# Earlier weight splits, three pieces a step beside the last routing, and exps ahead of the second tile's split

## The chip, the core and the metric

The kernel runs on one core of a Trainium2 chip. The metric is the time of one execution on the device, in microseconds (us), as the median of several runs. TensorE (PE) multiplies matrices, VectorE (DVE), ScalarE (ACT) and GpSimd (POOL) work on elements, and SP issues most of the DMA transfers, in the order in which they stand in its program, each when what it waits for is there.

## What is computed

Sliding-window attention over 4 sequences of 576 tokens, 8 heads of 64, then a mixture of 8 experts of which each token takes the two with the highest noisy logits, then a SwiGLU block behind an RMS norm. Cut to what matters here:

```python
scores = scale * np.matmul(q, k.transpose(0, 1, 3, 2))          # attention, window of 128
attn = np.exp(scores - max); attn = attn / attn.sum()
x = matmul(attn, v)                                             # 2304 tokens x 512
noisy_logits = x @ w_gate + np.log1p(np.exp(x @ w_noise)) * noise
top2 = np.argpartition(-noisy_logits, 2, axis=1)[:, :2]
for e in range(E):                                              # 8 experts
    h = np.maximum(x[mask] @ w1[e], 0.0)                        # 512 -> 1024
    out[mask] += top2_w[mask, k, None] * (h @ w2[e])            # 1024 -> 512
y = (silu(xn @ w_gate2) * (xn @ w_val) @ w_out)                 # xn: RMS norm of out
```

## The kernel before

The 2304 tokens are 18 tiles of 128. Float32 numbers go to TensorE as two float16 parts, a high one (a ScalarE copy) and a low one (a subtraction on VectorE or GpSimd); this is what "split" means below, for q and k of a tile (`split`, L262), for the result x (`split_x`, L379) and for the experts' weights (`weight_steps`, L98).

The attention loop (`while n < NS + HP + 2 ...`) runs in steps `n`, each one pair of heads of one tile: four steps a tile, 72 in all, from `n` = -2 on. A step writes out, for every engine in its order, the scores of steps `n + 2` and `n + 3` (TensorE L319, every second step), the turning of step `n`'s exps (L347), the products with v of step `n - 2` (L361), the exps of step `n + 1` (ScalarE L339), the shift and row minimum of step `n + 2` (VectorE L330), and beside them small work: loads of q, k and v (`load_qkv`, `load_v`), splits of tiles two ahead, `split_x` and `put_x` of a finished tile, logits (L458) and the routing of a batch of tiles (`route`, a generator that does one part a step: exp and ln, maxima and their indices, one-hots `m`, rank matmuls L495 and L497, then `slots`). The scheduler reorders nothing here (`manual_schedule`): each engine runs its instructions as the code writes them, and waits where something isn't ready.

When a batch is routed, `scatter` sends the tiles' rows with GpSimd's indirect DMA to `xrows`, sorted by expert. `take` (L525) waits until the tokens of its tiles are scattered, checks that the first expert has enough of them, and puts `rows` into the list `taking`: that generator lets `LANDS` steps pass and then issues the transposing reads of expert 0's rows (`row_steps`, L173). There are two takes: rows 0 to 255 behind tile 9, rows 256 to 383 behind tile 13.

`weights0` splits the first expert's weights inside attention: it is advanced at the steps in `WEIGHTS0`. The first three calls issue loads (L109), the next sixteen copy one half-piece each on ScalarE (L129) and subtract the one before on VectorE (L131), the last only subtracts (L134). `exp0` is the first layer of expert 0 for the two takes: 16 calls for the 256-wide block, 16 for the 128-wide one; each call issues six matmuls (L189), and every second one also a ScalarE relu (`hh`, L194) and a VectorE subtraction (`hl`, L195). From step 72 (`NS`) on two calls stand in each step, around the routing. What is left of `exp0` runs behind the loop, in `drive`, with the second expert's weights beside it.

`start` holds work for single steps at the beginning: here the second tile's split (k's low half on VectorE, q's on GpSimd) and the loads of the fourth tile.

Of the kernel before, what the change touches and what calls it, by code (L numbers as in the profile page):

```python
# [23 lines left out]
NEG = -1.0e9  # L24
CAP = 640

HELD, TURNED, LANDS = 8, 3, 4
MM = (3, 2)
VN = 96

# [11 lines left out]
def attention_moe_swiglu(  # L42
# [14 lines left out]
    nc = tc.nc  # L57
# [111 lines left out]
    def row_steps(e, cs, taken=None):  # L169
        if cs.start == 0:  # L170
            xts[e] = epool[e % 2].tile([P, 2 * KC, CAP], F16, name="xT")
        for c in range(cs.start, cs.stop, P):
            ins = nc.sync.dma_start_transpose(xts[e][:, :, c:c + P], xrows[e * N + c:e * N + c + P, :])  # L173
            if taken is not None:
                taken.append(ins)
            yield
# [45 lines left out]
    def expert_steps(e, *pieces):  # L222
        w1h, w1l, w2h, w2l = wts[e]
        steps = first_steps(hpool, w1h, w1l, xts[e], *pieces)
        hh, hl = next(steps)
        yield from steps
        for cs in pieces:
            for c in range(cs.start, cs.stop, P):
                yp = ps.tile([P, DM], F32, name="acc", bufs=2)
                yield from second_steps(yp, hh, hl, w2h, w2l, (c - pieces[0].start) // P)  # L230
                ys = yo.tile([P, DM], F32, name="ys")
                nc.scalar.activation(ys, yp, AF.Copy, scale=YSC)  # L232
                nc.sync.dma_start(ybuf[e * CAP + c:e * CAP + c + P, :], ys)
# [5 lines left out]
    with ExitStack() as actx:  # L239
# [9 lines left out]
        def load_qkv(t):  # L249
            raw[t] = io.tile([P, 2, HP, P], F32, name="raw", bufs=3)  # L250
            kq = qkv[t * P:(t + 1) * P, :2 * DM].rearrange("p (x g c) -> p x g c", x=2, g=HP)
            if t == 0:
                for gs in (slice(0, HP // 2), slice(HP // 2, HP)):
                    nc.sync.dma_start(raw[t][:, :, gs], kq[:, :, gs])
            else:
                nc.sync.dma_start(raw[t], kq)

        def load_v(t):
            v32[t] = io.tile([P, VW], F32, name="v32", bufs=6)
            nc.sync.dma_start(v32[t], qkv[t * P:(t + 1) * P, 2 * DM:])  # L260

        def split(t, x, lo, gs=slice(0, HP)):  # L262

            if x and t not in qT:
                qT[t] = work.tile([P, 2, HP, P], F16, name="qT", bufs=4)
            y = [qT[t][:, a, gs] if x else kT[:, a, gs, t % RING] for a in range(2)]
            nc.scalar.activation(y[0], raw[t][:, x, gs], AF.Copy)
            lo.tensor_tensor(out=y[1], in0=raw[t][:, x, gs], in1=y[0], op=OP.subtract)

        for t in range(3):  # L270
            load_qkv(t)
            load_v(t)

        rel = acons.tile([P, 2 * P], F32, name="rel")
# [28 lines left out]
        def scores(n):  # L303

            t = n // HP
            first = t * P % S == 0
            k0 = 1 if first else 0
            at = [(t - 1 + kk) % RING for kk in range(k0, 2)]
            chunks = ([(P, at[0], 1)] if first else [(0, at[0], 2)] if at[1] > at[0] else
                      [(0, at[0], 1), (P, at[1], 1)])  # L310
            for i in range(2):
                st[n + i] = dict(t=t, hp=(n + i) % HP, k0=k0, sp=ps.tile([P, 2, 2 * P], F32, name="mm0", bufs=MM[0]))
            for j in range(2):
                for c, sl, w in chunks:
                    for m, (a, b) in enumerate(((0, 0), (0, 1), (1, 0))):
                        for i in range(2):
                            h = heads((n + i) % HP)[j]
                            ds = slice(h % 2 * D, (h % 2 + 1) * D)
                            nc.tensor.matmul(st[n + i]["sp"][:, j, c:c + w * P], qT[t][ds, a, h // 2, :],  # L319
                                             kT[ds, b, h // 2, sl:sl + w, :], start=(m == 0), stop=(m == 2))  # L320
# [114 lines left out]
        def scatter(most):  # L435
            for t, i in todo[:most]:

                nc.gpsimd.memset(apart, 0)
                ins = nc.gpsimd.indirect_dma_start(
                    out=xrows[:, :], out_offset=bass.IndirectOffsetOnAxis(ap=slots[:, t, i:i + 1], axis=0),  # L440
                    in_=x16s[t].rearrange("p a d -> p (a d)"), in_offset=None)
                for o in scat:
                    tc.declare_no_dep(ins.ins, o.ins, reason="distinct rows")

                for o in early_reads:
                    tc.declare_no_dep(ins.ins, o.ins, reason="rows of earlier tokens")
                scat.append(ins)
                if i:
                    x16s.pop(t)
            del todo[:most]  # L450
# [74 lines left out]
        def take(i, tiles, cs):  # L525
            yield

            count = rt[:, NT, i * E:(i + 1) * E]
            nc.tensor.matmul(count, ones, mcum[0], start=True, stop=True)
            nc.vector.tensor_scalar(few[:, i:i + 1], count[:, 0:1], float(cs.stop), None, op0=OP.is_lt)  # L530
            while todo:
                scatter(2)
                yield

            def rows():
                for _ in range(LANDS):
                    yield
                yield from row_steps(0, cs, early_reads)
            taking.append(rows())
# [5 lines left out]
        def advance(steps):  # L545
# [5 lines left out]
                    del steps[0]  # L551

        start = {
            -2: [lambda: split(1, 0, nc.vector), lambda: split(1, 1, nc.gpsimd), lambda: load_qkv(3), lambda: load_v(3)],
        }
        weights0, weights1 = new_weights(0), new_weights(1)
        exp0 = expert_steps(0, *EARLY.values())
        NS = NT * HP

        WEIGHTS0 = (14, 15, 16, *range(18, 68, 3))  # L560
        WEIGHTS1 = range(NS - 2, NS + 1)
        n = -2
        while n < NS + HP + 2 or routing or ending or taking:
            t, p = divmod(n, HP)
            if 0 <= n + 2 < NS and n % 2 == 0:
                scores(n + 2)
            if 0 <= n < NS:
                turn(n)
            if 2 <= n < NS + 2:
                values(n - 2)  # L570
            if 0 <= n + 1 < NS:
                exps(n + 1)

            parts = [shift(n + 2)] if 0 <= n + 2 < NS else []
            if n % 2 == 0 and HP <= n < NS + 2:
                parts.append(divide((n - HP) // HP, (n - HP) // 2 % 2))
            if n == NS + 1:
                parts.append(divide(NT - 1, 1))
            for _ in itertools.zip_longest(*parts):
                pass  # L580
            if n >= NS:
                next(exp0, None)
                advance(routing)
                advance(ending)
                next(exp0, None)

            if 0 <= t < NT - 4 and p == 0:
                load_qkv(t + 4)
            if 1 <= t < NT - 3 and p == 0:
                load_v(t + 3)  # L590
            if 0 <= t < NT - 2 and p % 2:
                split(t + 2, p // 2, nc.gpsimd)
            for step in start.pop(n, ()):
                step()
            if p == (1 if t == NT else 3 if NT - 6 <= t - 1 < NT - 1 else 2) and 1 <= t <= NT:
                split_x(t - 1)
            if 0 <= n < NS:
                high(n)

            if p == (2 if t == NT else 3) and 1 <= t <= NT:  # L600
                put_x(t - 1)
            if n in (NS + 1, NS + 3) or p == 0 and 3 <= t < NT + 1:
                r = {NS + 1: NT - 2, NS + 3: NT - 1}.get(n, t - 3)
                logits(r)
                if r in batch_end:
                    (routing if r < NT - 1 else ending).append(route(*batch_end[r]))
                    if r + 1 in EARLY:
                        routing.append(take(list(EARLY).index(r + 1), r + 1, EARLY[r + 1]))
            advance(routing)
            advance(ending)  # L610
            advance(taking)
            if n > 2:
                advance(tasks)
            if p < 2 or n >= 60:
                scatter(1 if n < 68 else 2)
            if n in WEIGHTS0:
                next(weights0, None)
            if n in WEIGHTS1:
                next(weights1)
            n += 1  # L620
# [541 lines left out]
```

## Time and profile before

| | |
|---|---|
| three runs | 989.93, 991.82, 992.64 us, median 991.82 |
| the profiled execution | 997.68 us, of which 996.0 are the span from the first to the last instruction |
| TensorE busy | 955.9 us, 96% |
| VectorE, ScalarE, GpSimd busy | 656.4, 450.9, 212.0 us |
| attention and its end, to 177 us | TensorE busy with gaps; 100.00 of 100.00 us in 400 to 500 us |
| TensorE's granted clock, mean | 0.986 of full |

Times in the rows below count from the start of the span. A row of the timeline has start and duration, engine, line, operation, output<-input, the shape, a count where equal instructions are merged, and in brackets how long the engine was idle before it and what ended that. Durations of merged rows go from the first start to the last end. Ends of matmuls are modelled, so the distance between starts tells more than a duration. `hh`, `hl` are the first layer's result, `m` and `oh` one-hots of the routing, `pr` exps, `pf` the turned exps, `w1h`, `w2l` and so on weights, `st` loaded weights, `raw` loaded q and k.

### The profile page before, as it was taken

The page shows a single profiled execution, that of the slowest core. Times are in us where ns is not written, and L with a number is a line of the kernel's source. Part 1 is how long each engine was busy: PE and PEld are TensorE (multiplying, and loading weights), DVE is VectorE, ACT ScalarE, POOL GpSimd, SP SyncE. Part 2 cuts the span into 40 slices and gives each one's busy share as a digit, 9 for nine tenths or more (in the row PEclk, how much of TensorE's full clock was granted, in tenths as well). Part 3 has the DMA queues.
Part 4 walks back from the last instruction along what each step waited for, and adds up shares of the span by engine and source line. Part 5 has one row for each costly group of instructions (what it writes and reads, how often), then busy time and mean ns, then how long its engine had stood idle before and what let it go on. Part 6 is the DMA issues. An engine that isn't in the chain of part 4 may idle for free.

```text
span 996.0 us, 18517 instructions
## 1 busy us (share of the span) xinstructions
PE 955.9 (96%) x7220; PEld 667.4 (67%) x7220; DVE 656.4 (66%) x1503; ACT 450.9 (45%) x920; POOL 212.0 (21%) x255
## 2 busy tenths in 40 slices
PE   7999987999999999999999998889999999999997
PEld 5998885655656565656565685578478658847864
DVE  6688864537666666667675479989548917954850
ACT  8999852434454545454543335335323413432320
POOL 5467643000000000000001355541401140130000
PEclk9999988999999999999999998999999999999999
DMA  7999664748484757575750232311341070122000
GB/s 217 307 239 287 145 186 138 198 131 229 153 227 164 217 170 215 160 206 167 218 149 22 75 105 51 69 53 33 73 98 33 9 161 1 33 60 59 1 13 34
DMA packets 145279, 127.12 MB, mean 128 GB/s; under 512 B 97696, under 2 KB 114848, under 8 KB 145184
## 3 DMA queue, kind: packets, MB, share of 16 engines
q1 hardware_dynamic: 139424, 106.99, 40.1%
q0 software_dynamic: 5760, 18.88, 5.8%
q8 instruction: 58, 0.95, 0.4%
q14 instruction: 37, 0.30, 0.1%
HBM read 76.81 MB, written 26.74 MB: 104 GB/s over the span
## 4 chain that ended last, share of the span: by engine, by line
PE 86%; DVE 7%; ACT 2%; DMA 2%; issue 1%; SPq 1%; another core or an unknown queue 0%; DVEq 0%; ACTq 0%
PE acc L210 21%; PE mm L189 21%; PE mm L982 21%; PE acc L909 11%; PE acc L361 6%; PE mm L347 3%; DVE sums L933 3%; PE mm L319 2%; DMA xq<-xg 1%; SPq L838 1%; PE mm L875 1%; DVE pgl L891 1%; DMA raw<-in_qkv 1%; PE rt L458 1%
## 5 line engine op out<-in xcount | busy, mean ns | idle before, releaser
L189 PE MATMUL mm<-xT,w1h 128*128 128x256 f16 (+2 forms) x1088 | 167.1, 294 | 1.1 <-issue 0.8
L195 DVE SCALAR_TENSOR_TENSOR hl<-mm,hh 128x256 f16<-128x256 f32 (+2 forms) x136 | 63.5, 469 | 118.8 <-ACT hh L194 117.6
L189 PEld LDWEIGHTS <-w1h 128*128 128x128 f16 x1088 | 104.8, 99 | 41.2 <-issue 2.6
L210 PE MATMUL acc<-w2h,hh 128*128 128x512 f16 x320 | 121.3, 379 | 0.0
L210 PE MATMUL acc<-w2l,hh 128*128 128x512 f16 x320 | 121.3, 379 | 0.0
L210 PE MATMUL acc<-w2h,hl 128*128 128x512 f16 x320 | 121.3, 379 | 0.0
L939 POOL TENSOR_TENSOR sw<-sums,sw 128x256 f16<-128x256 f32 x36 | 28.4, 809 | 391.8 <-ACT sw L936 391.8
L210 PEld LDWEIGHTS <-hh 128*128 128x128 f16 x640 | 62.6, 98 | 72.8
L982 PE MATMUL mm<-xq,sw 128*128 128x256 f16 x864 | 100.4, 273 | 2.4 <-DMA xq<-xg 2.3
L194 ACT ACTIVATE hh<-mm 128x256 f16<-128x256 f32 (+2 forms) x136 | 56.6, 419 | 92.2 <-PE mm L189 86.2
L982 PEld LDWEIGHTS <-sw 128*128 128x128 f16 x864 | 84.3, 98 | 13.0 <-issue 2.7
L189 PE MATMUL mm<-xT,w1l 128*128 128x256 f16 (+2 forms) x544 | 93.1, 293 | 0.0
L909 PE MATMUL acc<-oh__3183,pgl 128*128 128x512 f16 (+2 forms) x228 | 83.3, 368 | 1.6 <-DVE pgl L891 1.6
L909 PE MATMUL acc<-oh__3183,pgh 128*128 128x512 f16 (+2 forms) x228 | 83.3, 368 | 0.4 <-ACT pgh L889 0.4
L909 PE MATMUL acc<-ol__3184,pgh 128*128 128x512 f16 (+2 forms) x228 | 83.3, 368 | 0.0
L909 PEld LDWEIGHTS <-pgh 128*128 128x128 f16 x456 | 44.0, 98 | 49.1 <-ACT pgh L889 0.7
L361 PE MATMUL acc<-v,pf 128*128 128x96 f32 x544 | 73.8, 277 | 2.6 <-issue 2.4
L361 PEld LDWEIGHTS acc<-v,pf 128*128 128x128 f32 x544 | 69.3, 197 | 2.4 <-issue 2.4
L189 PEld LDWEIGHTS <-w1l 128*128 128x128 f16 x544 | 52.5, 99 | 18.1
L339 ACT ACTIVATE pr<-ss,nm 128x256 f32<-128x256 f32 (+1 forms) x144 | 63.1, 488 | 3.2 <-DVE nm L330 2.1
L330 DVE CUSTOM_DVE_ANT_0 ss<-mm,bias 128x256 f32<-128x256 f32 (+1 forms) x144 | 54.2, 397 | 15.2 <-PE mm L319 6.7
L232 ACT ACTIVATE ys<-acc 128x512 f32<-128x512 f32 x40 | 23.8, 594 | 82.7 <-PE acc L210 74.2
(190 smaller groups left out, 1729.0 us busy)
## 6 DMA issues: line engine op xcount, KB each, us to landing
st<-in_moe_w SPq DMA_DIRECT2D x64, 512.0 KB, 4.9
ybuf<-ys SPq DMA_DIRECT2D x40, 256.0 KB, 3.0
raw<-in_qkv SPq DMA_DIRECT2D x17, 512.0 KB, 5.5
st<-in_moe_w_gate SPq DMA_DIRECT2D x12, 512.0 KB, 4.7
st<-in_moe_w_val SPq DMA_DIRECT2D x12, 512.0 KB, 4.3
st<-in_moe_w_out SPq DMA_DIRECT2D x12, 512.0 KB, 4.4
v<-in_qkv SPq DMA_DIRECT2D x18, 279.0 KB, 5.6
out<-ys SPq DMA_DIRECT2D x17, 256.0 KB, 2.1
```

The source lines that it names most:

```text
L189: nc.tensor.matmul(hp[:, :w], w1[:, c, f * P:(f + 1) * P], xT[:, xo + c, cs], start=(n == 0), stop=(n == 3 * KC - 1))
L194: nc.scalar.activation(hh[:, f, hs], hp[:, :w], AF.Relu)
L195: nc.vector.scalar_tensor_tensor(hl[:, f, hs], hp[:, :w], 0.0, hh[:, f, hs], op0=OP.max, op1=OP.subtract)
L210: nc.tensor.matmul(yp, hx[:, f, i * P:(i + 1) * P], w2[:, f, :], start=(n == 0), stop=(n == 3 * FC - 1))
L330: nc.vector.tensor_tensor_reduce(out=d["ss"][:, j, c0:], in0=d["sp"][:, j, c0:], in1=bias[kind][:, heads(d["hp"])[j], c0:], scale=-1.0 / K ...
L339: nc.scalar.activation(d["pr"][:, j, c0:], d["ss"][:, j, c0:], AF.Exp, scale=-1.0, bias=d["nm"][:, j:j + 1])
L347: nc.tensor.transpose(pt[:, j, kk, :], d["pr"][:, j, kk * P:(kk + 1) * P], ident)
L361: nc.tensor.matmul(xps[t, hp // 2][:, h % 4, :VN], ph[:, j, kk, :], v32[t - 1 + kk][:, h * DV:h * DV + VN], start=(kk == k0), stop=(kk == 1))
L909: nc.tensor.matmul(op[:, ds], px[:, f, cs], w[:, f, ds], start=(k == 0), stop=(k == 3 * GC - 1))
L933: nc.vector.tensor_tensor(out=o, in0=x, in1=y, op=op)
L939: nc.gpsimd.tensor_tensor(out=here[k][1], in0=x, in1=here[k][0], op=OP.subtract)
L982: nc.tensor.matmul(pp, w(a, pa, c), xq[:, 4 * b + 2 * pb + c, :], start=(n == 0), stop=(n == 5))
```

## The change

Four things are changed. The second take lets one step pass, not four, before it reads its rows. The q,k load of each of the first tiles goes ahead of the v load of the tile before. The second tile's split moves from step -2 to steps -1 (k) and 0 (q), with the fourth tile's loads at step 0. The weights' steps begin at 6, not 14, so that all end at step 57, not 66. And from step 74 on a third call of `exp0` stands at the end of each step.

```diff
-HELD, TURNED, LANDS = 8, 3, 4
+HELD, TURNED, LANDS = 8, 3, (4, 1)
...
+        load_qkv(0)
         for t in range(3):
-            load_qkv(t)
+            if t < 2:
+                load_qkv(t + 1)
             load_v(t)
...
             def rows():
-                for _ in range(LANDS):
+                for _ in range(LANDS[i]):
                     yield
...
         start = {
-            -2: [lambda: split(1, 0, nc.vector), lambda: split(1, 1, nc.gpsimd), lambda: load_qkv(3), lambda: load_v(3)],
+            -1: [lambda: split(1, 0, nc.vector)],
+            0: [lambda: split(1, 1, nc.gpsimd), lambda: load_qkv(3), lambda: load_v(3)],
         }
...
-        WEIGHTS0 = (14, 15, 16, *range(18, 68, 3))
+        WEIGHTS0 = (6, 7, 8, *range(9, 60, 3))
...
                 scatter(1 if n < 68 else 2)
+            if n > NS + 1:
+                next(exp0, None)
```

The changed code is a few lines longer, so its line numbers are 2 to 5 higher.

ScalarE at the start, before; `kT` and `qT` with 512 columns are the second tile's split, `pr` the exps of steps 0 and 1, then of step 2:

```order
L267 ACTIVATE kT<-raw 128x4x128
L267 ACTIVATE qT<-raw 128x512
L339 ACTIVATE pr<-ss,nm 128x128 x4
L352 ACTIVATE pf<-mm_212 128x2x128
L339 ACTIVATE pr<-ss,nm 128x128 x2
```

and now:

```order
L341 ACTIVATE pr<-ss,nm 128x128 x2
L267 ACTIVATE kT<-raw 128x4x128
L341 ACTIVATE pr<-ss,nm 128x128 x2
L267 ACTIVATE qT<-raw 128x512
L354 ACTIVATE pf<-mm_205 128x2x128
L341 ACTIVATE pr<-ss,nm 128x128 x2
```

The exps of step 0 stand ahead of both copies, those of step 1 between them.

VectorE about step 60, before; L372 to L376 divide a tile's half, L330 is the shift, L382 the cast of `split_x`:

```order
L374 RECIPROCAL rs<-rs 128x4
...
L376 TENSOR_TENSOR x<-acc,rs 128x256
L131 SCALAR_TENSOR_TENSOR w2l<-st,w2h 128x512
L330 ISA ss,nm<-mm_2448,bias_118 128x256
L330 ISA nm 128x1
...
L372 TENSOR_SCALAR rs<-acc 128x4
```

and now:

```order
L376 RECIPROCAL rs<-rs 128x4
...
L378 TENSOR_TENSOR x<-acc,rs 128x256
L332 ISA ss,nm<-mm_2453,bias_118 128x256
L332 ISA nm 128x1
...
L374 TENSOR_SCALAR rs<-acc 128x4
```

The subtraction of weights between the division and the shift is gone; in the same way it is gone behind the cast of step 63 and behind the maxima of step 66, and the copies on ScalarE at steps 57, 60 and 63.

VectorE beside the last routing batch (tiles 16 and 17), before; `hl` with 256 columns is the end of two calls of `exp0`:

```order
L195 SCALAR_TENSOR_TENSOR hl<-mm_3059,hh 128x256
L472 TENSOR_TENSOR ex<-ex,noise 128x16
L473 SCALAR_TENSOR_TENSOR nl<-rt,ex 128x16
...
L195 SCALAR_TENSOR_TENSOR hl<-mm_3093,hh 128x256
L481 COPY tops<-mx 128x4
...
L489 TENSOR_TENSOR m<-oh 128x16
L501 TENSOR_REDUCE msum<-m 128x8
L508 TENSOR_TENSOR m_3136<-m_3026,msum 128x8
L195 SCALAR_TENSOR_TENSOR hl<-mm_3124,hh 128x256
L513 TENSOR_TENSOR oh<-oh,rt 128x32
```

and now:

```order
L195 SCALAR_TENSOR_TENSOR hl<-mm_3060,hh 128x256
L195 SCALAR_TENSOR_TENSOR hl<-mm_3075,hh 128x256
L474 TENSOR_TENSOR ex<-ex,noise 128x16
...
L195 SCALAR_TENSOR_TENSOR hl<-mm_3109,hh 128x256
L483 COPY tops<-mx 128x4
...
L491 TENSOR_TENSOR m<-oh 128x16
L195 SCALAR_TENSOR_TENSOR hl<-mm_3139,hh 128x256
L503 TENSOR_REDUCE msum<-m 128x8
L510 TENSOR_TENSOR m_3159<-m_3027,msum 128x8
L515 TENSOR_TENSOR oh<-oh,rt 128x32
```

One `hl` more stands ahead of the routing's first part, one behind the one-hots instead of behind the sums; on TensorE one call of `exp0` (six matmuls) more stands ahead of the last logits, two more between these and the rank matmuls, one more behind them, and none of the 256-wide ones is left behind the loop.

## Rows read from the trace of the kernel before

**Rows 1.** Windows: stretch, length, busy us of PE, PEld, DVE, ACT, POOL, clock, DMA.

```profile
41.92:64.25 22.33, 22.33 (x271) 20.37 (x271) 19.13 (x94) 21.59 (x49) 11.73 (x13) 1.00 0.94 257
...
111.13:135.28 24.15, 20.35 (x238) 17.55 (x237) 21.42 (x85) 16.98 (x39) 15.88 (x22) 1.00 0.69 160
135.28:146.46 11.18, 11.18 (x105) 10.87 (x104) 6.30 (x29) 5.79 (x11) 5.13 (x9) 0.69 0.62 215
...
160.73:171.70 10.97, 7.56 (x72) 5.93 (x70) 5.31 (x27) 2.99 (x9) 6.41 (x14) 0.84 0.57 182
```

**Rows 2.** Timeline of the start: start, length, engine, line, instruction, idle before.

```profile
6.13 0.08 DVE L330 DVE_READ_ACCUMULATOR2_ANT nm<- 128x1 f32 x1
...
7.77 0.63 ACT L267 ACTIVATE kT<-raw 128x512 f16<-128x512 f32 x1 [2.57 <-DMA raw<-in_qkv]
...
8.82 1.26 ACT L339 ACTIVATE pr<-ss,nm 128x128 f32<-128x128 f32 x4
9.00 1.16 POOL L268 TENSOR_TENSOR qT<-raw,qT 128x512 f16<-128x512 f32 x1 [5.32 <-ACT qT L267]
...
9.35 1.26 PE L347 MATMUL mm<-ident,pr 128*128 128x128 f32 x4 [2.29 <-ACT pr L339]
```

**Rows 3.** Timeline of 119 to 135 us, and the group of line L131.

```profile
119.46 2.87 DVE L131 SCALAR_TENSOR_TENSOR w2l<-st,w2h 128x512 f16<-128x512 f32 x1
119.50 1.16 POOL L268 TENSOR_TENSOR qT<-raw,qT 128x512 f16<-128x512 f32 x1
...
120.58 0.83 PE L319 MATMUL mm<-kT,qT 64*128 64x256 f16 x12
...
122.25 0.41 DVE L330 CUSTOM_DVE_ANT_0 ss<-mm,bias 128x256 f32<-128x256 f32 x1
...
132.47 0.67 DVE L134 SCALAR_TENSOR_TENSOR w2l<-st,w2h 128x512 f16<-128x512 f32 x1
...
134.23 0.40 PE L394 MATMUL mm<-ident,x 128*128 128x128 f16 x4 [1.88 <-DVE x L382]
...
L131 DVE SCALAR_TENSOR_TENSOR w2l<-st,w2h x7: 674/686/2872, 87.8 to 127.0; 128x512 f16<-128x512 f32 x7
```

**Rows 4.** Window of an early stretch (as rows 1), and landings of tile raw.

```profile
23.64:34.53 10.89, 10.89 (x122) 9.81 (x122) 6.92 (x35) 9.89 (x23) 5.53 (x6) 1.00 1.07 269
...
DMA to landing us min/median/max: 2.9/4.7/8.0
```

**Rows 5.** Timeline beside the last routing batch.

```profile
161.04 0.60 PE L189 MATMUL mm<-xT,w1h 128*128 128x256 f16 x4
...
161.47 0.60 PE L189 MATMUL mm<-xT,w1l 128*128 128x256 f16 x4
...
164.07 0.38 ACT L194 ACTIVATE hh<-mm 128x256 f16<-128x256 f32 x1 [1.78 <-remote]
...
165.55 0.18 PE L495 MATMUL rt<-m,tri 128*128 128x8 f16 x1 [2.39 <-DVE m L489]
...
167.53 0.17 PE L625 MATMUL rt<-m,ones 128*128 128x8 f16 x1 [1.02 <-DVE oh L513]
...
171.04 0.82 PE L189 MATMUL mm<-xT,w1h 128*128 128x256 f16 x8
```

**Rows 6.** Timeline: scatters on POOL, SP's transposing reads, and these reads' landings.

```profile
149.46 0.96 POOL L439 DMA_INDIRECT xrows<-x,slots  x1 [0.22 <-issue]
...
163.66 0.96 POOL L439 DMA_INDIRECT xrows<-x,slots  x1 [0.22 <-issue]
...
166.38 1.24 SPq L173 DMA_TRANSPOSE xT<-xrows  x1
...
176.58 3.03 SPq L173 DMA_TRANSPOSE xT<-xrows  x2
...
DMA to landing us min/median/max: 3.7/3.9/4.2
```

**Rows 7.** Timeline: a wait of ACT that nothing in the profile ends.

```profile
119.77 0.60 ACT L352 ACTIVATE pf<-mm 128x512 f32<-128x512 f32 x1 [3.05 <-remote]
```

## The prediction

> **What bounds the kernel now.** I read the page first, then busy time by stretch, then the timelines of the three places that the change touches, then the waits of TensorE. Steps below are the values of `n` of the attention loop; a piece is one `next(exp0)`, six 128x256 matmuls of the first expert. Behind the attention part TensorE works nearly throughout, by positions in its own work and not by the hour, so what attention gains comes through to the end. In attention TensorE is the bound too while all goes well: in 41.92 to 64.25 it is busy 22.33 of 22.33 us, although four weight splits fall there, with ScalarE at 21.59 [rows 1]. So splits in a steady stretch are free. Three places are not like that. At the start TensorE waits 2.29 us for the first exps [rows 2]. In 111.13 to 135.28 it is busy 20.35 of 24.15, and VectorE 21.42 [rows 1]. In 160.73 to 171.70, beside the last tiles' routing, it is busy 7.56 of 10.97 [rows 1].
>
> **Start: exps ahead of the second tile's splits, second q,k load ahead of the first v.** ScalarE now idles 2.57 us until the second tile's load lands at 7.77, copies k and q of it and only at 8.82 computes four exps [rows 2], although their shifted scores were there at 6.21 [rows 2]. Now two of the exps (half of the 1.26 us, 0.63) go into that idle time. The load is issued one transfer earlier; its landing can move from nothing to somewhat over a microsecond, and I take nothing. But q's low half on GpSimd (1.16 us, from 9.00) stands before the third pair of scores on TensorE, and q's copy now stands behind two more exps; if the load lands no earlier, q's half comes about 0.5 us later. So from -0.5 to 1.2 us; ScalarE has no idle time there afterwards, so I take the middle of it, 0.5.
>
> **Middle: three of the splits move from steps 60, 63, 66 to steps 9, 12, 15** (the loads from 14, 15, 16 to 6, 7, 8; the steps between keep one split every third step). This takes from VectorE the low-half instruction at 119.46, which took 2.87 us, one of the usual 0.68 us, and the last at 132.47, 0.67 us [rows 3]; from ScalarE three copies. The first held back the shift that follows, which began at 122.25 though its scores ended at 121.41 (120.58 and 0.83): 0.8 us [rows 3]. The last stands right before the shift and the cast for which TensorE waited 1.88 us at 134.23 [rows 3]; without it and the lag carried there that wait shrinks by 0.67 to 1.35, I take 0.8. Sum 1.6; the ends are 0.7 (the last instruction alone) and 3.8, all that TensorE idles in the stretch (24.15 less 20.35). What is late next at 134.23 is the cast itself, behind the routing's maxima on VectorE, so about a microsecond of that wait stays. After it the granted clock was at half level (1.2 GHz) in most of 135.28 to 146.46, mean 0.69 [rows 1]; at 11.18 us times 0.31 that costs 3.4 us. I leave that loss in the forecast, since some wait stays.
>
> In the early steps the added work meets cover: VectorE is busy 6.92 and ScalarE 9.89 of 10.89 us in 23.64 to 34.53 [rows 4]. Two splits there add 1.24 us to ScalarE, 0.24 too many, and the whole early stretch, some 16 us, could lose 0.4; the earlier stretch with logits runs at 97% ScalarE without loss, so I count nothing. The instruction of 2.87 us ran while GpSimd did two subtractions from 119.50 on, and the median of its kind is 0.686 [rows 3]. The Trainium skill (SBUF — State Buffer, SBUF: two separate sides) says that a VectorE instruction with two SBUF inputs and a GpSimd one exclude each other, whichever starts first. By that rule, which the row bears out, the moved splits meet GpSimd's splits early as well, at up to 2.2 us each, two in 10.89 us where VectorE has 3.97 idle: at worst 0.6 us back in all, and 5.3 instead of 5.9 in the sum below.
>
> **End: three pieces a step from step 74 on, and the second take lands after 1 step instead of 4.** Four pieces come sooner: one before the last tile's logits (160.73), two between these and the rank matmul, one behind that. A piece is six matmuls at a quarter of 0.43 us each (from 161.04 to 161.47), 0.65 us [rows 5]. Now TensorE waits 2.39 us at 165.55 for the one-hots and 1.02 us at 167.53 for the ranks; and the four pieces left run behind them, partly at half level, until 171.47 (171.04 and four matmuls of the eight there): 3.9 us instead of 2.6 [rows 5]. So 10.4 us pass from 161.04 to 171.47, of which eight pieces are 5.2. What the routing needs: from the logits to the last wait 167.53 less 160.73, 6.8 us. The piece ahead of the logits delays them by 0.65. If the chain stays as long, it ends at 168.2 and no wide piece is left: gain 3.3. If the halves that VectorE subtracts are no longer waited for in the second part of the chain (now ScalarE starts one at 164.07, 1.78 us after it was idle, and the one-hots stand behind it [rows 5]), TensorE is never short but for about 0.7 us: gain 4.3. If the additional subtractions stand in the chain's way by 1.5 us, 1.8. I take 3.8.
> For this the third block of rows has to be there. Now its transposing read is issued at 166.38, 1.76 us behind the end of the scatter of 163.66 to 164.62, and lands 3.9 us later, at 170.3 [rows 6]: with that, the 128-wide pieces could not start before 170.3 and the gain would be 1.2. With one step of waiting it stands in the program before the scatters of tiles 14 and 15 and waits for the one of 149.46 (ends 150.42): issue at about 152.2, there at 156.1, eleven microseconds early. On SP's queue the loads behind it move forward with it. The next rows, for the last 256 tokens, are issued at 176.58 [rows 6] and used behind three tiles' second stage of TensorE, 72 matmuls of 512 columns, which begin some 4 us sooner than now: still some 6 us behind the landing, so covered.
>
> **Sum.** 0.5 + 1.6 + 3.8 = 5.9 us. The profiled execution took 997.68 us (span 996.0 and 1.7 around it): 991.8. The runs' median is 991.82, 5.9 below the profiled one, so some of the waits counted may be shorter there; I take the difference over unreduced: **985.9 us**.
>
> **Rivals.**
> *The clock stays up.* If the shorter wait at 134.23 leaves the clock at 2.4 GHz, the 3.4 us come on top: 982.5. For: the fall followed that wait. Against: a microsecond of it stays. Chance 0.22.
> *The routing chain remains the limit* and the additional subtractions lengthen it: end 1.8 instead of 3.8, and the middle at its low end of 0.7: 991.82 less 3.0, 988.8. For: ScalarE and VectorE take things in order, and a half subtraction now stands ahead of the one-hots as before. Chance 0.16.
> *The waits only move.* Before 119.77 ScalarE stands still for 3.05 us with nothing in the profile that releases it late [rows 7], while GpSimd scatters; the 1.78 us before 164.07 are put down in the same way [rows 5]. The change doesn't touch these, and if such a stall takes the place of the waits filled, the gain is 0 to 3: 990.5. Chance 0.13.
> *Slower: loads crowd the early DMA queues.* Three loads of 512 KB go out between 16 and 27 us, where the DMA share is 1.07 at 269 GB/s [rows 4]: 1.95 us each, 5.9 us in all for whatever is queued behind. A q,k load lands after 4.7 us in the median, 8.0 at most [rows 4], and is used nine steps after its issue, at 22.33 us for twelve steps [rows 1] some 16.7 us. 8.0 + 5.9 = 13.9 is under that, so it should be hidden; from 16.7 us on ScalarE would stand at the copy, with every exp behind it. Two such loads 5 us late: 985.9 + 10 = 996. Chance 0.07.
> The forecast itself has 0.42.
>
> **Numbers.** About 0.3%, 3.0 us, is what a measurement of this kernel can tell from no change. The forecast with its own bounds is 984 to 988, all faster, as is the rival with the clock; of the chain rival about three quarters. Faster 0.76, the same 0.17, slower 0.07. Range 981 to 991: it takes in the clock rival with a microsecond and a half, the chain rival and half of the moved waits; outside lie the slow case and the rest, under 0.2.
>
> **What the profile after would show.** First wait of TensorE for an exp under 2 us, third scores no later than 10.6. No split behind step 57, and in the stretch that was 111 to 135 TensorE idle for 2 us less; the wait for the cast about 1 us. The third row read issued near 152; one wait for one-hots under 1 us and none for ranks; the 128-wide pieces some 6 us earlier than 171.5. Wrong: if a wait of ScalarE for the weights' or q,k loads shows in the first 40 us, if the rank matmul comes later than 166.5 by the old clock of the steps, or if the gain sits beyond 190 us.

## The result, and the profile after

The changed kernel takes 983.71 us in the median of ten runs, the kernel before 992.74 beside it; the ratio is 0.9906, with a 95% interval from 0.9891 to 0.9921. That is 9.3 us (7.8 to 10.8) less, where 5.9 were forecast. The profiled execution took 982.35 us, with a span of 980.6.

First the windows beside those of [rows 1]: the steady stretch, the one up to the score block at 135.25, the 11.18 us that follow it, and the stretch from the last logits to the first product with `w1l` of the 128-wide block (159.26 here, 171.70 before). The third has the length of its counterpart, not its work; the others are placed by TensorE's own work. Columns: stretch, length, busy us of PE, PEld, DVE, ACT, POOL, granted clock, DMA share, GB/s.

```profile
42.73:65.06 22.33, 22.33 (x271) 20.37 (x270) 19.43 (x98) 21.60 (x49) 12.07 (x13) 1.00 0.93 260
111.94:135.25 23.31, 20.87 (x238) 18.76 (x238) 16.01 (x82) 15.64 (x36) 15.19 (x22) 0.93 0.70 166
135.25:146.43 11.18, 11.18 (x141) 10.71 (x140) 6.82 (x32) 7.29 (x15) 6.01 (x11) 1.00 0.65 229
153.36:159.26 5.90, 5.43 (x66) 4.70 (x64) 4.20 (x23) 1.60 (x6) 3.79 (x9) 1.00 0.91 285
```

The steady stretch is the same to the hundredth. In the third TensorE is busy throughout, as before, but 141 matmuls go through where [rows 1] have 105: the clock is full, not 0.69. In the fourth TensorE idles 0.47 us (5.90 less 5.43), where [rows 1] have 3.41, and the clock is full, not 0.84. In the second it idles 2.44 us, where [rows 1] have 3.80, and the clock, 1.00 before, is 0.93.

The start after the change, in the timeline (start, length, engine, line, instruction, idle before and what ended it):

```profile
6.12 0.69 ACT L341 ACTIVATE pr<-ss,nm 128x128 f32<-128x128 f32 x2 [0.82 <-DVE nm L332]
6.73 0.63 ACT L267 ACTIVATE kT<-raw 128x512 f16<-128x512 f32 x1
...
9.76 1.03 PE L321 MATMUL mm<-kT,qT 64*128 64x256 f16 x8 [0.62 <-POOL qT L268]
...
10.60 0.84 SPq L256 DMA_DIRECT2D raw<-in_qkv  x2
...
13.37 1.46 PE L321 MATMUL mm<-kT,qT 64*128 64x256 f16 x12
...
17.28 0.83 PE L321 MATMUL mm<-kT,qT 64*128 64x256 f16 x12
17.72 0.63 ACT L267 ACTIVATE kT<-raw 128x512 f16<-128x512 f32 x1 [0.35 <-DMA raw<-in_qkv]
...
35.34 0.28 PE L321 MATMUL mm<-kT,qT 64*128 64x256 f16 x2
```

The 2.29 us for the first exps of [rows 2] are gone (in the second profile of this kernel, below, 1.02 us of such a wait are left); instead TensorE waits for q's low half on GpSimd (0.62), and ScalarE for the fourth tile's load (0.35).

The middle:

```profile
119.33 0.96 POOL L441 DMA_INDIRECT xrows<-x,slots  x1 [0.22 <-issue]
...
120.31 1.16 POOL L268 TENSOR_TENSOR qT<-raw,qT 128x512 f16<-128x512 f32 x1
...
121.53 0.67 PE L321 MATMUL mm<-kT,qT 64*128 64x256 f16 x8 [1.79 <-POOL qT L268]
...
134.19 0.40 PE L396 MATMUL mm<-ident,x 128*128 128x128 f16 x4 [0.32 <-DVE x L384]
```

The cast is waited for by 0.32 us, where [rows 3] have 1.88. Ahead of it stands a wait that the first trace of before doesn't show: the low half of tile 16's q, behind scatters on GpSimd. Behind that wait the granted clock is at half level, up to 190 us in this window only:

```profile
121.95:125.37 3.42, 3.42 (x20) 3.25 (x17) 2.20 (x11) 1.91 (x4) 3.01 (x6) 0.50 0.56 44
```

The end, beside [rows 5] and [rows 6]:

```profile
150.17 0.17 PE L497 MATMUL rt<-m,tri 128*128 128x8 f16 x1 [1.57 <-DVE m L491]
...
151.45 1.24 SPq L173 DMA_TRANSPOSE xT<-xrows  x1
...
157.57 0.18 PE L497 MATMUL rt<-m,tri 128*128 128x8 f16 x1 [0.47 <-ACT hh L194]
...
159.01 0.17 PE L630 MATMUL rt<-m,ones 128*128 128x8 f16 x1
159.04 0.38 PE L189 MATMUL mm<-xT,w1h 128*128 128x128 f16 x4
```

The third block of rows is read at 151.45, ahead of the last batch's rank matmul TensorE waits 0.47 us (the row names a relu on ScalarE; the one-hots were ready 0.02 us before it), the ranks are not waited for at all, and the 128-wide pieces begin at 159.04, directly behind.

### The profile page after: what moved, and what is told of

It reads as the page before. It is cut to its first block, busy times and chain, and to the rows that moved or that the text cites. A ratio compares the mean times of both kernels' runs of the same rounds, so it can differ in the third digit from the quotient of the medians.

```text
span 980.6 us, 18518 instructions
## 1 busy us (share of the span) xinstructions
PE 950.8 (97%) x7220; PEld 663.9 (68%) x7220; DVE 652.7 (67%) x1503; ACT 450.3 (46%) x920; POOL 212.9 (22%) x255
## 4 chain that ended last, share of the span: by engine, by line
PE 87%; DVE 7%; DMA 2%; ACT 1%; issue 1%; POOL 1%; SPq 1%; DVEq 0%; ACTq 0%; POOLq 0%
PE acc L210 21%; PE mm L189 21%; PE mm L987 21%; PE acc L914 11%; PE acc L363 6%; PE mm L349 4%; DVE sums L938 3%; PE mm L321 3%; DMA xq<-xg 1%; SPq L843 1%; DVE pgl L896 1%; PE rt L460 0%; PE mm L880 0%; DVE ya L770 0%; DMA yb<-ybuf,ysl 0%
## 5 line engine op out<-in xcount | busy, mean ns | idle before, releaser
L189 PE MATMUL mm<-xT,w1h 128*128 128x256 f16 (+2 forms) x1088 | 164.8, 291 | 0.0
L189 PEld LDWEIGHTS <-w1l 128*128 128x128 f16 x544 | 52.1, 98 | 17.7
```

The costliest lines, as they stand in the source:

```text
L189: nc.tensor.matmul(hp[:, :w], w1[:, c, f * P:(f + 1) * P], xT[:, xo + c, cs], start=(n == 0), stop=(n == 3 * KC - 1))
```

## The experiments

Medians below are of 6 to 12 runs each. The first four kernels ran on one chip (before: 991.03), the next four on another (991.31), the last four on a third (999.80), so each is compared with the kernel before on its own chip, by the ratio. The changed kernel itself ran beside the second four only; its 983.71 (0.9906) is that of the result.

**The start undone.**

```
-        load_qkv(0)
         for t in range(3):
-            if t < 2:
-                load_qkv(t + 1)
+            load_qkv(t)
...
+            -2: [lambda: split(1, 0, nc.vector), lambda: split(1, 1, nc.gpsimd), lambda: load_qkv(3), lambda: load_v(3)],
```

> The changed kernel with the start put back as it was (loads in the old order, second tile's split at step -2). Theory A, read from the trace after: the new start costs time, since the third scores wait 0.62 us for q's low half on GpSimd and the matmuls stay at half rate longer; the block of step 14 then begins at about 34.5 us instead of 35.34 and the time falls by 0.8 us against the changed kernel, to about 982.9 (ratio to before 0.9898). Theory B, as predicted: the new start gains 0.5, so undoing it gives 984.2 (0.9911). Theory C: the block of step 60 waits for GpSimd anyway, and nothing changes (within 0.3 us).

(The blocks that the expectations call those of step 14 and 60 are written by the code in steps 16 and 62.) Measured: 983.12, ratio 0.9916 (0.9897 to 0.9934). In the profile the block stood at 34.65, as Theory A has it, but TensorE then waited 0.98 us at 44.34 for the transposed x, and the score block that waits for GpSimd came at 122.01, not sooner than the 121.53 above: Theory C in effect, though by another wait than it names. By the medians the three theories can't be told apart, the interval being 1.8 us to either side.

**The second take waits four steps again.**

```
-HELD, TURNED, LANDS = 8, 3, (4, 1)
+HELD, TURNED, LANDS = 8, 3, 4
```

> The changed kernel with LANDS 4 for the second take again. Theory A, as predicted: the third row read then waits for the scatters of tiles 14 and 15, which end at 157.5 in the trace after, is issued near 159.3 and lands near 163.2; the first 128-wide piece, now at 159.04, waits some 4 us: 987.8 (0.9948). If the granted clock falls behind that wait, up to 1.7 us more. Theory B: the third piece gives the gain by itself, and the landing hides behind pieces still left: within 0.5 us of the changed kernel.

Measured: 989.67, ratio 0.9976 (0.9960 to 0.9993), where the changed kernel has 0.9906: 6 us slower by the medians, 7 by the ratios. In the timeline and the windows:

```profile
158.73 1.30 SPq L173 DMA_TRANSPOSE xT<-xrows  x1
...
162.34 0.58 PE L189 MATMUL mm<-xT,w1h 128*128 128x128 f16 x4 [4.03 <-DMA xT<-xrows]
```

```profile
162.34:165.56 3.22, 3.22 (x31) 3.22 (x31) 0.45 (x2) 0.74 (x3) 0.58 (x1) 0.50 0.98 321
```

The wait is 4.03 us and the half level comes right behind it. Theory A, with its surcharge: without the earlier read three quarters of the change's gain are gone (0.24% is left of 0.94).

**Two pieces a step.**

```
-            if n > NS + 1:
-                next(exp0, None)
```

> The changed kernel without the third piece a step (LANDS stays 1 for the second take). Theory A, as predicted: four pieces of 0.65 us leave the routing's waits; the waits for the one-hots and ranks of the last batch come back to about 2.4 and 1.0 us: some 3 us slower than the changed kernel, 986.7 (0.9937), and up to 2 us more if the granted clock falls again beside the last routing as before the change. Theory B: the end gained because the rows landed sooner and the clock stayed up after the cast, not by the third piece: within 1 us of the changed kernel.

Measured: 985.71, ratio 0.9933 (0.9915 to 0.9952), 2.0 us slower than the changed kernel's 983.71 and 3.0 than its 982.75 in the second measurement. The waits are back at 0.86 for the last one-hots and 1.02 for the ranks; the one-hots' is smaller than the 2.4 expected, which came from the first trace of before. Theory A, at two thirds of its 3 us or all of it.

**The weights' steps alone.**

```
-        WEIGHTS0 = (14, 15, 16, *range(18, 68, 3))
+        WEIGHTS0 = (6, 7, 8, *range(9, 60, 3))
```

> The kernel before with the weights' steps alone begun at 6. Theory A, as predicted: 1.6 us come off in 111 to 135 us, 991.1 (0.9984). Theory B, read from the trace after: TensorE gets to the block of step 60 about 2 us sooner but then waits about 1.8 us for q's low half on GpSimd, behind the scatters; about 0.8 us are left of it. In both the question is the granted clock behind the cast at 134: if it stays at full level as in the trace after, 3.4 us more come off, 987.7 to 988.5 (0.995).

Measured: 988.04, ratio 0.9967 (0.9952 to 0.9981). The wait for GpSimd is there (1.79 us), the one for the cast is 0.32, and the clock is full from 126.50 to 164.05. Ahead of 163.40 TensorE waits 2.10 us for the third block of rows, which this kernel reads as late as before, and the half level follows. Theory B with the clock: 3.0 us.

**The kernel before once more**, for a second profile.

> The kernel before, unchanged, for a second profile. The first profiled execution took 997.68 us, 5 to 7 above the medians of 991.0 and 992.7. Theory A: the surplus lies beside the routing, in the idle stretches of 148.5 to 151.8 us that nothing in the profile ends (2.1 us) and in the half-level clock of 136.1 to 143.0 and 166.8 to 170.3 us (up to 5.1 us in all), so an execution of 991 to 992 us lacks most of these. Theory B: these are in every execution and the surplus lies behind 190 us.

Measured: 991.86, the profiled execution 991.29. Theory A in the main. None of the idle stretches that nothing ends is there, and up to 190 us the half level covers two stretches of 3.4 us, not 13.7 us in all; but TensorE's waits are others than in the first trace:

```profile
121.83 0.61 PE L319 MATMUL mm<-kT,qT 64*128 64x256 f16 x8 [2.07 <-POOL qT L268]
130.16 0.81 PE L319 MATMUL mm<-kT,qT 64*128 64x256 f16 x11 [0.89 <-DVE nm L330]
135.85 0.40 PE L394 MATMUL mm<-ident,x 128*128 128x128 f16 x4 [2.12 <-DVE x L382]
153.71 0.17 PE L495 MATMUL rt<-m,tri 128*128 128x8 f16 x1 [1.79 <-DVE m L489]
161.19 0.18 PE L495 MATMUL rt<-m,tri 128*128 128x8 f16 x1 [0.86 <-DVE m L489]
163.17 0.17 PE L625 MATMUL rt<-m,ones 128*128 128x8 f16 x1 [1.02 <-DVE oh L513]
166.48 0.38 PE L189 MATMUL mm<-xT,w1h 128*128 128x128 f16 x4 [0.50 <-DMA xT<-xrows]
```

The two half-level stretches, in its windows:

```profile
137.40:140.81 3.41, 3.41 (x32) 2.99 (x28) 2.19 (x12) 2.81 (x6) 0.00 (x0) 0.50 0.65 215
154.46:157.88 3.42, 3.42 (x22) 2.69 (x21) 1.27 (x6) 1.40 (x2) 1.29 (x3) 0.50 0.00 0
```

**The changed kernel once more**, beside it.

> The changed kernel, unchanged, beside the others of this call. Both theories: 982 to 985 us. Theory A: the 1.79 us wait for q's low half near 120 and one half-level stretch behind it are there again. Theory B: they belong to the one profiled execution.

Measured: 982.75, ratio 0.9907 (0.9884 to 0.9929); the wait for GpSimd is 1.79 us again, with one half-level stretch behind it (122.26 to 125.68). Theory A. The profiles of these two runs, 991.29 and 983.37 us, are what the account below goes by; it calls them the second pair. Windows of before (up to the block at 35.36, to 115.49, to 136.90, to the first second-layer matmul at 171.83), then of the changed kernel to the same places:

```profile
0.00:35.36 35.36, 27.54 (x274) 23.45 (x274) 22.98 (x109) 28.71 (x67) 17.96 (x29) 1.00 0.83 225
35.36:115.49 80.13, 79.75 (x992) 72.28 (x992) 66.40 (x332) 75.39 (x173) 52.28 (x62) 1.00 0.94 254
115.49:136.90 21.41, 15.99 (x189) 14.00 (x189) 17.82 (x73) 14.36 (x33) 12.29 (x17) 1.00 0.64 167
136.90:171.83 34.93, 30.68 (x360) 27.37 (x359) 21.99 (x95) 16.32 (x39) 17.04 (x31) 0.90 0.51 176
```

```profile
0.00:35.97 35.97, 29.30 (x274) 23.96 (x274) 23.74 (x111) 29.61 (x69) 17.97 (x29) 1.00 0.87 245
35.97:116.09 80.12, 79.74 (x991) 72.29 (x992) 67.71 (x334) 75.24 (x173) 53.14 (x62) 1.00 0.90 243
116.09:135.87 19.78, 17.33 (x189) 15.24 (x189) 15.08 (x70) 13.44 (x31) 12.05 (x17) 0.91 0.57 154
135.87:165.03 29.16, 27.11 (x361) 25.07 (x360) 20.18 (x93) 15.15 (x37) 17.26 (x31) 1.00 0.63 214
```

The four lengths differ by +0.61, -0.01, -1.63 and -5.77, in sum -6.8; the rest of the 7.9 between the two executions lies behind, in the later stages, whose waits differ between the two.

**Tile 16's q on VectorE.**

```
-                split(t + 2, p // 2, nc.gpsimd)
+                split(t + 2, p // 2, nc.vector if n == NS - 13 else nc.gpsimd)
```

> The changed kernel with the low half of tile 16's q subtracted on VectorE, not on GpSimd, where it stands behind six scatters (one more VectorE instruction of about 0.69 us ahead of a cast). Theory A: TensorE's wait of 1.79 us at 119.7 goes, and with it the half-level stretch of 3.4 us behind it, worth 1.7: 983.7 less 3.5, 980.2 (ratio to before 0.988). Theory B: the wait goes but a half-level stretch comes behind the next wait, at the one-hots near 149: 982.0 (0.990). Theory C: VectorE is late by as much and nothing changes, 983.7.

Measured: 982.71, ratio 0.9896 (0.9876 to 0.9916), against 982.75 of the changed kernel beside it. The wait of 1.79 us is gone, and the half level has moved behind the next one, the 1.57 us for the one-hots at 148.62:

```profile
149.21:152.63 3.42, 3.42 (x23) 2.62 (x21) 1.27 (x6) 1.40 (x2) 1.05 (x2) 0.50 0.38 92
116.64:133.69 17.05, 15.74 (x189) 13.98 (x188) 13.68 (x71) 13.33 (x31) 10.77 (x16) 1.00 0.59 168
133.69:164.43 30.74, 28.77 (x361) 26.05 (x359) 20.12 (x93) 15.15 (x37) 17.23 (x31) 0.94 0.62 209
```

The first window is the half-level stretch. The middle is 2.7 us shorter than the 19.78 above, the end 1.6 longer than the 29.16. Theory B by its mechanism; of the 1.7 us that it leaves, the medians show nothing. In this profile TensorE also waited 0.83 us ahead of 46.03 for the transposed x, a wait that neither profile of the changed kernel has.

**The end's two edits alone.**

```
+HELD, TURNED, LANDS = 8, 3, (4, 1)
...
+            if n > NS + 1:
+                next(exp0, None)
```

> The kernel before with the end's two edits alone: the third piece a step and LANDS 1 for the second take. Theory A, as predicted: 3.8 us come off beside the last routing, and nothing ahead of it moves: 991.0 less 3.8, 987.2 (0.9962). Theory B: the gain beside the last routing is only whole when the clock stays up behind the cast at 134, which this kernel still waits for by 1.9 us: about 2 us, 989 (0.998).

Measured: 986.92, ratio 0.9944 (0.9925 to 0.9963), 4.4 us off the 991.31. Theory A on the median; Theory B's concern shows in the profiled execution (988.50), where the half level stood for 10.2 us in this part and the end came out only 1.2 us shorter than before.

**Two more pieces, with tile 16's q on VectorE; the same with the second tile's q too; that alone; the start alone.** These four ran on the third chip.

```
-            if n > NS + 1:
+            if n >= NS:
...
-            0: [lambda: split(1, 1, nc.gpsimd), lambda: load_qkv(3), lambda: load_v(3)],
+            0: [lambda: split(1, 1, nc.vector), lambda: load_qkv(3), lambda: load_v(3)],
```

> The changed kernel with tile 16's q subtracted on VectorE (as in the run before this one) and the third piece a step from step 72 on, two steps earlier, so that two more pieces (1.3 us) stand ahead of the one-hots for which TensorE waited 1.57 us at 148.6. Theory A: that wait shrinks to about 0.3 us and the half-level stretch behind it (3.4 us, worth 1.7) stays away: 982.7 less 3.0, 979.7 (ratio to before 0.988). Theory B: the half-level stretch comes behind another wait all the same: 981.4 (0.990). Theory C: the pieces' subtractions lengthen the routing's chain and the wait stays: 982.7.

> The same with the second tile's q low half on VectorE too. Theory A: the wait of 0.62 us for the third scores at about 10 us goes and everything behind comes 0.6 us sooner, or more if the matmuls reach full rate sooner: 979.1 (0.9875). Theory B: VectorE's shifts stand behind the subtraction and the next exps are late by as much: as without it, 979.7.

> The changed kernel with only the second tile's q low half moved from GpSimd to VectorE. Theory A: the 0.62 us wait for the third scores goes and with the start 0.7 us sooner than now the time falls by 0.6 to 0.7: 982.5. Theory B: the gain shows at step 14 but the wait for GpSimd near 120 swallows it: 983.2, no change.

> The kernel before with the new start alone. Theory A, read from the traces: everything up to 118 us comes 0.7 us later than in the kernel before, by the wait for q's low half and the longer half rate: 991.3 plus 0.7, 992.0 (1.0007). Theory B, as predicted: 0.5 us sooner, 990.8 (0.9995). Theory C: the waits near 120 take up whichever, 991.3.

Measured, in this order: 994.19 (ratio 0.9943, 0.9925 to 0.9962), 994.10 (0.9939, 0.9921 to 0.9957), 997.43 (0.9965, 0.9952 to 0.9979) and 999.69 (0.9999, 0.9987 to 1.0012), with 999.80 before. The absolute times expected don't hold on this chip, and the changed kernel itself didn't run on it. Of the first kernel's theories none is shown: the wait of 1.57 us is gone from its profile, but the half level stands from 150.4 to 157.2, behind stalls that the last section shows, and the last one-hots are waited for by 2.94 us. Moving the second tile's q as well changes nothing that these medians can tell (994.19 against 994.10, with intervals of nearly 2 us to either side), though the wait of 0.62 us is gone. The start alone is at no difference, but its interval of 1.3 us takes in all three theories. With two more pieces and tile 16's q the medians are 3.2 and 3.3 us under that of the third kernel (997.43). Whether that holds where before takes 991, these runs don't tell.

## Why the prediction was right, and where it was not

**The sum.** 5.9 us were forecast and about 9 came. Middle and end hold the gain, as foretold; of the single parts the start alone gave nothing, the weights alone 0.33%, the end alone 0.56%, and their sum is the whole's 0.9%. That forecast and result are so near is in part luck, since errors of the terms cancelled, as the next paragraphs show.

**Start, +0.5: the wrong sign in the trace, nothing in the time.** The two exps went into the idle time and the third scores came at 9.76 (10.62 in the second pair), about as written. The second tile's load even landed 0.6 to 1.0 us sooner (copy of its k at 6.73 and 7.59 us, before at 7.77 and 8.18), where the sum took nothing. The step that failed is the one that looked no further than the waits for the second tile. TensorE's idle time up to 35 us did fall, from 7.82 (35.36 less 27.54) to 6.67 us, but the same 274 matmuls took 29.30 us, not 27.54: in the first trace after, the twelve scores at 13.37 still took 1.46 us and only those at 17.28 took 0.83, while before the change 0.83 is reached at 13.97:

```profile
10.55 1.46 PE L319 MATMUL mm<-kT,qT 64*128 64x256 f16 x12
...
13.97 0.83 PE L319 MATMUL mm<-kT,qT 64*128 64x256 f16 x12
```

Why they ran at the lower rate for longer isn't shown; the windows' clock column reads 1.00 there. And a later limit stands behind it, the fourth tile's load. ScalarE's copy of its k (17.72 here) stands 17.61 or 17.62 us ahead of the block at 35.34 in all nine profiles with the new start, so that what holds it back holds back the rest; in eight of them it waits for the landing itself, by 0.2 to 1.4 us. In the five with the old start the distance is 17.74 or 17.75 us and the copy waits for no landing. The row at 10.60 above is two loads: step 0 of the loop issues the fifth tile's load (`load_qkv(t + 4)`) before it comes to `start`, so that the fourth tile's, moved there by the change, goes out second, at 11.08, and lands 6.6 us later, at 17.7. In the second trace of before it went out first, at 11.27, and landed 5.7 us later, 0.6 us ahead of its copy at 17.61. So faster exps only meet a later wait; whether the old order of these two loads would mend it was not tried. A wait of ScalarE for a q,k load in the first 40 us is what the prediction named as a sign of being wrong, and the slower rival had it, for 10 us; here it belongs to a difference of 0.6. The weights' loads, which that rival blamed, are not the cause: the kernel with the start alone, whose weights come late, waits 0.44 us at the same copy.

**Middle, 1.6: 1.63 measured, but put together otherwise, and so by luck.** In the first pair of profiles the block at 135.28 comes at 135.25 after: 0.8 us lost at the start, 0.8 regained. In the second pair, by the windows, TensorE's idle time fell from 5.42 (21.41 less 15.99) to 2.45 us, and its busy time rose by 1.34 at a granted clock of 0.91. (Foretold were 2 us less of idle time; the first pair has 1.4, the second 3.0.) The step that failed is "a microsecond of that wait stays" for the cast: it is 0.32. The step that was missing is the queue of GpSimd. In the first trace the score block came at 120.58, just as q's low half was done ([rows 3]: 119.50 and 1.16), so nothing waited; TensorE had stood still shortly before, for 0.96 us up to 120.40, with nothing in the profile that ends it. In the second trace of before, and after, it is there earlier and waits 2.07 and 1.79 us for the low half. GpSimd's row is the clue that the prediction read only for what it did to VectorE.

**The early cover held.** No split behind step 57 is left. The three that moved up took 0.68, 1.19 and 0.68 us on VectorE (at 30.0, 35.0 and 41.7 in the first trace after), and the stretch from 35.36 to 115.49 and its counterpart are equal. Four of the other kernels with early weights, though, waited 0.5 to 1.0 us for the transposed x at 44 to 46 us, none of those with late weights and neither profile of the changed kernel; why was not tried. The late split that went was dearer than the first trace had it (4.54 us, not 2.87). From the second trace of before:

```profile
124.74 4.54 DVE L131 SCALAR_TENSOR_TENSOR w2l<-st,w2h 128x512 f16<-128x512 f32 x1
...
125.34 1.16 POOL L268 TENSOR_TENSOR kT<-raw,kT 128x512 f16<-128x512 f32 x1
126.46 1.16 POOL L268 TENSOR_TENSOR qT<-raw,qT 128x512 f16<-128x512 f32 x1
...
127.57 1.15 POOL L384 TENSOR_TENSOR x<-x,x 128x512 f16<-128x512 f32 x1
```

It lasted until 129.28, past three subtractions of GpSimd. The Trainium skill (SBUF — State Buffer, SBUF: two separate sides) says that a VectorE instruction with two SBUF inputs and a GpSimd one exclude each other, and that whichever starts first holds the other off. The first half fits these rows, since VectorE's took 4.54 us in place of 0.68 while GpSimd's took their usual 1.16; the second doesn't, since by these rows VectorE's began first. Of the 0.6 us that the prediction allowed for this in the early steps, at most 0.5 came (1.19 less 0.68).

**End, 3.8: 5.8 between the two profiles, 4.4 in the kernel that has it alone.** What was foretold stands: the read near 152 (151.45), one wait for one-hots under 1 us (0.47; the 1.57 us of the batch before it stay as they were), none for ranks. The 128-wide pieces, foretold some 6 us earlier, begin 12.4 us earlier in the first pair (159.04) and 6.8 in the second. The wait without the earlier read is the 4.03 us of the second experiment. Idle time fell by 2.2 us (34.93 less 30.68, against 29.16 less 27.11). The other 3.6 are the clock: the same matmuls, busy 30.68 and 27.11 us, at 0.90 and 1.00; half of that lies behind the cast, so with the middle's edit. The sum's largest wait, 2.39 us for the one-hots, was the first trace's: in the second one it is 0.86. So the term is near its size partly by luck: it took that wait at what one execution showed, and the clock, whose loss the forecast left in, made up for it.

**The clock rival.** It had 0.22, at 3.4 us on top of the forecast, 982.5, and it is nearest to what came: two half-level stretches (137.40 to 140.81 and 154.46 to 157.88) went, of 1.7 us each in TensorE's time, though only the first stands behind the cast. Against that one came behind the wait for GpSimd, at 1.3 to 1.7 us. All executions outside the third chip say the same: the granted clock over the span is 0.990 in the median before, and 0.995 in both measurements of the changed kernel. One less that clock, times spans of 989 and 981 us, makes a loss of some 9.9 and 4.9 us (by the means 9.0 and 5.0). So, as an estimate from these clocks, 4 to 5 of the 9 us came by the clock and the rest by waits. The step that mis-sized the forecast is leaving all of the loss in since "some wait stays": up to 190 us, in the traces of the first two chips, the half level followed waits of 1.57 us and more, and behind the cast's 0.32 it did not come. It doesn't follow each wait of that size, though: behind the 1.57 us ahead of 150.17 the changed kernel kept its clock, and the kernel with tile 16's q on VectorE lost it behind the same wait. Of the eight profiles with the wait of 1.79 to 2.07 us for GpSimd it fell behind it in four. On the third chip it also fell behind rows of stalls of which none is over 1.1 us. When it comes is not settled by these runs, so a single profile can't price it.

**The moved waits** may be the case of the third chip, where a kernel with all of the change and one instruction moved gains 2.4 us by the medians (3.5 by the ratio), about that rival's 0 to 3. The changed kernel itself was not measured there, so this isn't shown.

## What to carry to other kernels

Where TensorE is the bound but for a few waits, a wait is worth its length and, in the executions where the clock falls behind it, some 1.7 us more (half of a 3.4 us stretch here): filling it with work that is ready (pieces of another stage) pays both, if the data of that work is asked for early enough. A trace shows only the waits that came last in that execution; before costing a removed one, follow every queue to its next item, here GpSimd's scatters ahead of a subtraction and, on SP, the fifth tile's load ahead of the fourth's. Where one execution is 5 us above the median, take a second one before its waits are summed.

## What the runs showed that was not expected

In the first trace of before and in all four of the third chip TensorE stands still for up to 1.1 us at a time, with nothing in the profile that ends it, while GpSimd issues scatters back to back. From the kernel with two more pieces, TensorE and GpSimd:

```profile
145.92 0.96 POOL L441 DMA_INDIRECT xrows<-x,slots  x1 [0.21 <-issue]
...
146.57 0.59 PE L363 MATMUL acc<-v,pf 128*128 128x96 f32 x4 [0.69 <-issue]
...
147.19 0.96 POOL L441 DMA_INDIRECT xrows<-x,slots  x1 [0.21 <-issue]
...
148.03 0.59 PE L363 MATMUL acc<-v,pf 128*128 128x96 f32 x4 [0.87 <-issue]
...
148.45 0.96 POOL L441 DMA_INDIRECT xrows<-x,slots  x1 [0.21 <-issue]
...
149.48 0.38 PE L189 MATMUL mm<-xT,w1l 128*128 128x256 f16 x2 [0.86 <-issue]
```

The scatters take 0.96 us and come every 1.27 us as in the other traces, where TensorE runs through beside them (5.92 of 6.00 us busy from 146 to 152 in the second trace of before, 3.01 here). ScalarE and VectorE do less too (0.97 and 0.61 us busy, where the second trace of before has 2.08 and 2.99). The third chip's kernel before is 8 to 9 us slower than on the other two; its granted clock is 0.983 in the median, where theirs is 0.990, which is some 7 us of it by the estimate above (17.0 less 9.9). What stops TensorE there was not found.
